# A decode block that streams its K and V cache: fourteen of the loads issued from ScalarE's queue

## The chip, the cores and the metric

The kernel runs on one core of a Trainium2 chip. A core has a matrix engine (TensorE, PE in the profile), a vector engine (VectorE, DVE), an activation engine (ScalarE, ACT), a general engine (GpSimd, POOL) and a sequencer that computes nothing (SyncE, SP). Each follows its own list of instructions in order, and they wait for each other by semaphores. Transfers between the memory of the chip (DRAM) and the core's on-chip memory are carried out by 16 DMA engines. An instruction of SP, ScalarE or GpSimd only issues a transfer; the engines do the rest. The profile tells by queue whose transfers they are: q1 holds those that SP issues, q10 those of ScalarE, q0 those of GpSimd.

The metric is the device time of one execution in microseconds, as the median of several runs.

## The reference

Two tokens (batch 2, one position each) go through an attention block that reads a cache, and then through an MLP.

```
h  = x  + attention(layernorm(x))
h2 = h  + mlp(layernorm(h))

attention: q = x @ wq                     # 512 -> 32 heads x 128
           scores = (q . k_cache) / sqrt(128)   # k_cache: 2 x 32 x 8192 x 128, fp32
           p = softmax(scores)
           o = p . v_cache                # v_cache: 2 x 32 x 8192 x 128, fp32
           o @ wo                         # 4096 -> 512
mlp:       layernorm, 512 -> 1792, gelu, 1792 -> 512, biases
```

The two caches hold 268 MB each. Everything else is small beside them: wq and wo have 8.4 MB each, the weights of the MLP 7.3 MB together.

## The kernel before

The work on the cache is cut into 32 rounds, i = 0 to 31. A round is one batch row and two heads; both heads are laid over the 128 partitions, so that a partition holds 128 keys of one head, 128 numbers each, 64 KB. One load of K, or of V, is thus 128 rows of 64 KB, 8.39 MB. There are 64 of them. They share a pool `kv` of three buffers with wq, which is loaded first; later, the weights of the MLP use the pool too. In the order of the program the buffers are taken by wq, K0, V0, K1, V1, K2 and so on, each load going into the buffer of the one three places ahead of it: V(i) takes the buffer of K(i-1), and K(i+1) takes that of V(i-1).

A round's K is worked on in four chunks. VectorE multiplies a chunk with the query in place (`multiply`, L246). GpSimd adds the two halves of each row (`halve`, L256), and VectorE sums what is left (`sums`, L266). In the last three rounds ScalarE sums some of the rows (`by_act`, L260); before those it has nothing to do there. After the fourth chunk VectorE takes the row maximum (`row_max`, L270). In the next round the maximum goes over TensorE and VectorE to all partitions (`all_max`, L273, L277, L280), ScalarE takes the exponentials (`exps`, L286 and L291), and TensorE multiplies them with V (`values`, L314, 64 matmuls). ScalarE copies the result from PSUM (`gather`, L320), TensorE sums it over partitions (`head_sum`, L335), and VectorE divides by the sum and sorts it into rows (`head_out`, L350). When the heads of a group of rows of wo are complete, they are multiplied with that group (`turned`, L367).

Two of the waits matter here. The load of V(i) is issued when the last sums over K(i-1) are done. The load of K(i+1) is issued when the matmuls over V(i-1) are done.

Within a round the program issues, in this order: the load of V(i) (L394); the exponentials, the matmuls over V of the round before; the load of K(i+1) (L409); in some rounds a group of wo (L414, `load_wo`); the four chunks, with `gather` behind the first. The list of a queue follows this order.

The groups of wo share one buffer. A group is loaded by SP (L140) or, where its rows are not evenly laid out, by GpSimd with an indirect DMA (L145), and the one behind it waits until the matmuls at L367 have used it. In the rounds that matter here SP loads one, at i = 9, and GpSimd one, at i = 13; GpSimd's group before that was loaded at i = 5.

All loads of K and V are issued by SP. ScalarE issues a single transfer, that of x at the start (L66).

Of the kernel before, what the change touches and what calls it, by code (L numbers as in the profile page):

```python
# [37 lines left out]
FAR = 4096  # L38


@with_exitstack
def tile_decode_block(ctx: ExitStack, tc: tile.TileContext, x, k, v, wq, wo, w1, b1, w2, b2, out):
    nc = tc.nc
# [23 lines left out]

    def load(src, i, parts):  # L70
        m, b = divmod(i, B)
        t = kv.tile([P, NS, DH], F32, name="kv", tag="kv")
        rows = src[b, QG * m:QG * m + QG].rearrange("h (p j) d -> (h p) j d", j=NS)
        for s0, n in parts:
            nc.sync.dma_start(t[:, s0:s0 + n], rows[:, s0:s0 + n])
        return t

    wqt = kv.tile([P, DC, H * DH], F32, name="wqs", tag="kv")
# [16 lines left out]
    for blocks in PLAN:  # L95
        shut = blocks if isinstance(blocks, tuple) else None
        r = WR if shut else blocks
        n = (P - 4 * len(shut or ())) * r
# [13 lines left out]
    for _, _, _, blocks in groups:  # L112
        if blocks and blocks not in index:
# [3 lines left out]
            for p in sorted(set(ends)):  # L117
                if ends.count(p) == 1:
                    if p in blocks:
                        edge, step, first = p, FAR, p  # L120
                    else:
                        edge, step = p, first - p - FAR
                    one = work.tile([P, 1], F32, name="ix1")
# [261 lines left out]
    next_load = 0  # L385
    free_from = 1
    kt[0] = load(k, 0, cut(1))
    for i in range(NI):
        m, b = divmod(i, B)
        done = i - 1  # L390
        late = i == NI - 1
        if not late:
            if i < NI - 2:
                vt[i] = load(v, i, cut(1))  # L394
        else:
            vt[i] = load(v, i, [(0, 64), (64, 32), (96, 24), (120, 8)])
            b1r = rows2[:, 0].rearrange("p r q -> p (r q)")[:, :FN]
            nc.vector.memset(b1r, 0.0)
            b2s = rows2[:B, 1].rearrange("b r q -> b (r q)")
            for e in range(B):  # L400
                nc.sync.dma_start(b1r[WB * e::32], b1.rearrange("(n f) -> n f", n=NG))
            nc.sync.dma_start(b2s, b2[None, :].to_broadcast([B, D]))
# [248 lines left out]
```

## Time and profile before

| what | value |
|---|---|
| median of 3 runs | 1307.52 us (1307.45 to 1307.59) |
| span of the profiled execution | 1305.9 us |
| bytes moved by DMA | 561.50 MB |
| mean rate over the span | 430 GB/s |
| VectorE busy | 932.7 us |
| GpSimd busy | 494.2 us |
| TensorE busy | 446.8 us |
| ScalarE busy | 98.6 us |

The profile is one execution. Its span goes from the first to the last instruction; the time of a run has 1.6 us more, by the median. In the lists of groups and waits a line like L246 is a line of the kernel. In the timeline a row gives the start in us, the duration in us, the engine, the line, the operation, and the tiles written and read; `x2` says that two instructions are merged, and the bracket gives the idle time before it and what ended it. `SPq` and `ACTq` are the queues' own instructions, the issuing of a transfer among them. In the DMA view a queue's row gives packets, MB and share of the 16 engines' time in the window.

### The profile page before, as it was taken

Reading aid. Unit: us, or ns where it says so; the run is one execution under the profiler, and the core shown is the slowest. Engines: PE = TensorE matmul, PEld = TensorE weight load, DVE = VectorE, ACT = ScalarE, POOL = GpSimd, SP = SyncE. Lnnn points to the kernel's source line nnn. Section 1 sums busy time; section 2 is a strip of 40 time slices with the busy share of each in tenths; the row PEclk is TensorE's granted clock in tenths of the full one; section 3 lists DMA queues with packets and bytes.
Section 4 is the critical chain, followed back from the end, with each engine's and each line's share of the span. In section 5 each row is a group of like instructions: output and inputs, shape, how many; then the busy total and the mean of one; then the engine's idle time right before and its main releaser. Section 6 shows DMA issues by size and latency. Waiting matters only on the chain.

```text
span 1305.9 us, 7466 instructions
## 1 busy us (share of the span) xinstructions
PE 446.8 (34%) x2934; PEld 130.9 (10%) x2934; DVE 932.7 (71%) x551; ACT 98.6 (8%) x431; POOL 494.2 (38%) x151
## 2 busy tenths in 40 slices
PE   3033313333332334413342232333323334123468
PEld 0001001010010101001010010101001011000113
DVE  3666688757688666787766787666787667797891
ACT  0000000000000000000000000000000000004440
POOL 0433344532344432444332454333444433453330
PEclk9566556766566666656766566666666666566689
DMA  9999999999999999999999999999999999999998
GB/s 418 426 440 428 438 422 444 424 440 426 442 426 440 428 438 428 426 444 430 436 426 438 430 434 436 424 442 424 440 426 432 438 432 436 429 428 429 428 434 351
DMA packets 12727, 561.50 MB, mean 430 GB/s; under 512 B 1568, under 2 KB 1584, under 8 KB 2484
## 3 DMA queue, kind: packets, MB, share of 16 engines
q1 hardware_dynamic: 11968, 557.08, 98.8%
q0 software_dynamic: 720, 3.93, 0.7%
q8 instruction: 23, 0.38, 0.1%
q14 instruction: 12, 0.10, 0.0%
q10 hardware_dynamic: 4, 0.00, 0.0%
HBM read 562.32 MB, written 0.00 MB: 431 GB/s over the span
## 4 chain that ended last, share of the span: by engine, by line
DMA 43%; DVE 24%; issue 14%; PE 12%; POOL 5%; ACT 1%; SPq 0%; POOLq 0%; DVEq 0%
DMA kv<-in_A_k_cache_dram 38%; DVE kv L246 14%; PE so L314 10%; DVE s L266 9%; POOL kv L256 5%; DMA kv<-in_A_v_cache_dram 3%; DMA ws<-in_B_w_dram 1%; ACT pt L291 1%; PE rowacc L367 1%; DVE orow L350 1%; PE sm L280 1%; PE sm L273 0%; DVE gm L277 0%; DVE mx L270 0%; ACT nb L286 0%
## 5 line engine op out<-in xcount | busy, mean ns | idle before, releaser
L246 DVE TENSOR_TENSOR kv<-kv,qps 128x4096 f32<-128x4096 f32 x128 | 562.4, 4415 | 313.8 <-DMA kv<-in_A_k_cache_dram 313.6
L256 POOL TENSOR_TENSOR kv<-kv 128x2048 f32<-128x2048 f32 (+3 forms) x128 | 476.8, 3734 | 754.1 <-DVE kv L246 566.3
L266 DVE TENSOR_REDUCE s<-kv 128x32 f32<-128x2048 f32 (+5 forms) x160 | 325.3, 2066 | 10.9 <-POOL kv L256 10.6
L314 PE MATMUL so<-kv,pt 128*8 128x512 f32 x2048 | 280.8, 709 | 42.7 <-ACT pt L291 37.3
L273 PE MATMUL sm<-ident,mx 128*1 128x128 f32 x32 | 10.9, 340 | 446.0 <-DVE mx L270 446.0
L314 PEld LDWEIGHTS so<-kv,pt 128*8 128x8 f32 x2048 | 56.4, 101 | 239.5 <-issue 194.3
L367 PE MATMUL rowacc<-wog,ot 128*2 128x512 f32 x70 | 50.3, 881 | 64.8 <-DVE ot L365 33.4
L286 ACT ACTIVATE nb<-sm 128x2 f32<-128x2 f32 x32 | 5.5, 172 | 851.4 <-PE sm L280 851.4
L231 PE MATMUL qps<-q,pick 2*64 2x256 f32 x64 | 13.8, 577 | 127.6 <-DVE kv L246 127.6
L273 PEld LDWEIGHTS sm<-ident,mx 128*1 128x1 f32 x32 | 2.5, 79 | 472.5 <-issue 278.0
L358 PE MATMUL sm<-ident,orow 2*128 2x2 f32 x35 | 5.2, 244 | 130.1 <-DVE orow L350 130.1
L320 ACT ACTIVATE ss<-so 128x512 f32<-128x512 f32 x31 | 18.5, 598 | 269.6 <-PE so L314 269.6
L260 ACT ACTIVATE kv<-kv 128x128 f32<-128x128 f32 x114 | 33.5, 295 | 24.2 <-DVE kv L246 21.4
L335 PE MATMUL sm<-ss,selr 128*34 128x128 f32 x240 | 28.7, 273 | 0.0
L291 ACT ACTIVATE pt<-s,nb 64x128 f32<-64x128 f32 x64 | 25.5, 399 | 1.4
L335 PEld LDWEIGHTS sm<-ss,selr 128*34 128x34 f32 x240 | 25.1, 112 | 0.0
L260 ACT ACTIVATION_READ_ACCUMULATOR kv<-kv 128x1 f32 x114 | 21.3, 186 | 0.0
L280 PE MATMUL sm<-gm,ones 1*128 1x2 f32 x64 | 16.6, 326 | 11.9 <-DVE gm L277 11.9
L277 DVE TENSOR_REDUCE gm<-sm 1x2 f32<-1x128 f32 x32 | 8.9, 279 | 16.2 <-PE sm L273 16.2
L231 PEld LDWEIGHTS qps<-q,pick 2*64 2x64 f32 x64 | 5.5, 192 | 136.9 <-DVE kv L246 133.2
L358 PEld LDWEIGHTS sm<-ident,orow 2*128 2x128 f32 x35 | 4.4, 207 | 132.6 <-DVE orow L350 79.9
L367 PEld LDWEIGHTS rowacc<-wog,ot 128*2 128x2 f32 x70 | 6.8, 107 | 97.9 <-issue 64.1
(110 smaller groups left out, 169.2 us busy)
## 6 DMA issues: line engine op xcount, KB each, us to landing
kv<-in_A_k_cache_dram SPq DMA_DIRECT2D x4, 4096.0 KB, 32.9
ws<-in_B_w_dram SPq DMA_DIRECT2D x3, 1792.0 KB, 18.5
kv<-in_A_v_cache_dram SPq DMA_DIRECT2D x1, 4096.0 KB, 33.4
wog<-in_A_wo_dram SPq DMA_DIRECT2D x3, 1024.0 KB
kv<-in_A_v_cache_dram SPq DMA_DIRECT2D x1, 2048.0 KB, 37.9
kv<-in_A_v_cache_dram SPq DMA_DIRECT2D x1, 1536.0 KB, 41.2
ws<-in_B_w_dram SPq DMA_DIRECT2D x1, 1024.0 KB, 17.0
wog<-in_A_wo_dram SPq DMA_DIRECT2D x1, 512.0 KB
```

What stands on the lines that cost most here:

```text
L231: nc.tensor.matmul(t[e * HP:(e + 1) * HP, :, b], pick[32 * n:32 * n + B, b, :], rows[:, :, e], start=True, stop=True)
L246: return nc.vector.tensor_tensor(kc, kc, qb, op=ALU.mult)
L256: nc.gpsimd.tensor_tensor(t[:, :, :DH // 2], t[:, :, :DH // 2], t[:, :, DH // 2:], op=ALU.add)
L260: nc.scalar.activation(kt[i][:, j, :], kt[i][:, j, :], AF.Copy, accum_out=ST[i][:, j:j + 1])
L266: nc.vector.tensor_reduce(ST[i][:, a:e], kt[i][:, a:e, :d], axis=AX.X, op=ALU.add)
L273: nc.tensor.transpose(MT[i], mx, ident)
L280: GI[i] = nc.tensor.matmul(GM[i], ones[:1, :], gm, start=True, stop=True)
L291: nc.scalar.activation(ptz[i % 2][ps, :, 4 * e:4 * e + 4], s[ps], AF.Exp, bias=nb[ps, e:e + 1], scale=SCALE, accum_out=LT[m][ps, 32 * e + ...
L314: m = nc.tensor.matmul(so[32 * n:32 * n + 4 * QG], ptz[i % 2][:, u, :], vt[i][:, 4 * u:4 * u + 4, :], start=(u < NG), stop=(u >= NS // 4 - ...
L320: return nc.scalar.activation(SS[i], so2[i % 2], AF.Copy)
L335: nc.tensor.matmul(OP[m], sel_row[:, j, B - 1 - c:B - 1 - c + QR], SS[i - 1 + c][:, j * DH:(j + 1) * DH], start=(c == 0 and j == 0), stop= ...
L367: nc.tensor.matmul(rowacc, t[:, r, :], wo_g[g][:, r, :], start=False, stop=(g == len(groups) - 1 and r == n - 1))
```

## The change

The function `load` counts its calls. Calls 13 to 26, counted from 0 in the order of the program, issue their transfer on ScalarE's queue; all others issue it on SP's, as before. The calls are K0, V0, K1, V1, ..., so that numbers 13 to 26 are V6, K7, V7, K8, ..., V12, K13: seven loads of V and seven of K. Each of them is one transfer of the whole 8.39 MB. Nothing else is changed: buffers, order of the program and waits are the same.

```
+BY_ACT = range(13, 27)
...
+    loads = [0]
+
     def load(src, i, parts):
         m, b = divmod(i, B)
         t = kv.tile([P, NS, DH], F32, name="kv", tag="kv")
         rows = src[b, QG * m:QG * m + QG].rearrange("h (p j) d -> (h p) j d", j=NS)
+        queue = nc.scalar if loads[0] in BY_ACT else nc.sync
+        loads[0] += 1
         for s0, n in parts:
-            nc.sync.dma_start(t[:, s0:s0 + n], rows[:, s0:s0 + n])
+            queue.dma_start(t[:, s0:s0 + n], rows[:, s0:s0 + n])
         return t
```

## The prediction

> **What bounds the kernel now.** I read the page from the top: first the busy shares, then the slices of DMA, then who waits for whom, and then single loads in the timeline.
>
> ```profile
> span 1305.9 us, 7466 instructions
> DMA  9999999999999999999999999999999999999998
> q1 hardware_dynamic: 11968, 557.08, 98.8%
> 20.00:1290.00 1270.00, 434.09 (x2736) 124.57 (x2736) 918.05 (x439) 94.28 (x425) 492.88 (x142) 0.65 1.00 432
> DVE kv L246 <- DMA kv<-in_A_k_cache_dram: 313.6, 31, 28.5
> SPq L75 <- DVE mx L270: 764.5, 28, 29.7
> ```
>
> The fourth line is a view by stage, from 20 to 1290 us: its last two columns are the DMA share and GB/s. The 16 DMA engines are busy for 1.00 of the stage and move 432 GB/s, nearly all of it on q1, the ring that SP feeds. VectorE is busy for 918 of 1270 us and waits 313.6 us for K, about 10 us in each of 31 rounds. So the bytes bound the kernel, and a change can cost time only where the engines run empty, or gain where the same bytes move faster. SP is no bound: its longest wait is for VectorE to free a buffer. (I name the row maximum that its wait is put down to; the issue comes as the last sum over K ends.)
>
> Unit prices follow from this. A load of K or V is 128 rows of 64 KB, 8.39 MB: at 432 GB/s 19.4 us, eight packets on each of 16 engines, 2.43 us each. The load that meets empty rings at the start of the run is dearer:
>
> ```profile
> 0.74 0.40 SPq L79 DMA_DIRECT2D wqs<-in_A_wq_dram  x1
> 0.74 0.54 ACTq L66 DMA_DIRECT2D x<-in_A_x_dram  x1
> wqs<-in_A_wq_dram SPq DMA_DIRECT2D x1, 22.5
> q10 hardware_dynamic: 4, 0.00, 6.2%
> ```
>
> Wq has the size of one load and takes 22.5 us from issue to landing, 3.1 us more than in a full stream. The last line is from the DMA view of 1.6 to 1.8 us: the four packets of x, ScalarE's only transfer (ring q10), start there, about 0.9 to 1.0 us after their issue at 0.74.
>
> **The change, part by part.** Counted in program order, loads 13 to 26 are V6, K7, V7 and so on to V12 and K13. Removed from SP: 14 issues of 0.33 us, 4.6 us. SP waits hundreds of us, so this gains nothing. Added to ScalarE: the same 14, at 0.33 to 0.54 us. What stands behind each on ScalarE:
>
> ```profile
> 267.46 0.33 SPq L75 DMA_DIRECT2D kv<-in_A_v_cache_dram  x1
> 269.25 0.17 ACT L286 ACTIVATE nb<-sm 128x2 f32<-128x2 f32 x1 [26.99 <-PE sm L280]
> 279.39 0.33 SPq L75 DMA_DIRECT2D kv<-in_A_k_cache_dram  x1
> 279.40 0.60 ACT L320 ACTIVATE ss<-so 128x512 f32<-128x512 f32 x1 [8.94 <-PE so L314]
> ```
>
> V6 would be issued at 267.46; the next ScalarE instruction can start only at 269.25, when the maximum has come back from TensorE, so the issue is covered by 1.8 us of idle time. K7 and the gather at L320 are released together by the same matmuls; the gather goes 0.33 to 0.54 us later, and its PSUM bank is overwritten only by the values two rounds later, a round being some 39 us. Nothing, then, in either case. The waits keep their order too: on ScalarE the buffer of a V load comes free before the exponentials of that round, and that of a K load just before the gather, so no instruction is queued behind a later event than before.
>
> What is left is that q1 and q10 both hold loads at two places: K6 (SP) with V6 (ScalarE), and K13 (ScalarE) with V13 (SP). On one ring a load waits for the one ahead of it. On two rings the trace shows what happens when GpSimd's ring q0 gets 8 KB rows of Wo while q1 is full:
>
> ```profile
> 232.77 1.16 POOL L145 DMA_INDIRECT wog<-in_A_wo_dram,ix  x1 [0.28 <-POOL wog L144]
> DMA packets 32, 1.11 MB, mean 398 GB/s; under 512 B 8, under 2 KB 8, under 8 KB 8
> q1 hardware_dynamic: 16, 1.05, 86.4%
> q0 software_dynamic: 16, 0.07, 5.7%
> ```
>
> The last three lines are the DMA view of 239.2 to 242.0 us. In 2.8 us, the time of one 64 KB and one 8 KB packet, q1 starts 16 packets and q0 starts 16: one of each on 16 engines. The rings take turns packet by packet, and q0 does not wait for q1's queued load. So with equal packets V6 takes half of the engines' time from K6.
>
> The Trainium skill (DMA: Bandwidth & Descriptors, Queues, rings and completion order) says that each DMA engine goes round robin over the queue rows, and that it drains a whole packet, roughly 9 to 17 descriptors, before it switches. The trace agrees on the turns; but here a turn is a single 64 KB row. By packets of nine descriptors an engine's eight rows of K6 would be one turn, K6 would not be delayed, and the sum would be 0.
>
> ```profile
> 280.83 8.75 DVE L246 TENSOR_TENSOR kv<-kv,qps 128x4096 f32<-128x4096 f32 x2 [12.25 <-DMA kv<-in_A_k_cache_dram]
> 310.16 0.33 SPq L75 DMA_DIRECT2D kv<-in_A_v_cache_dram  x1
> 310.16 0.29 DVE L270 TENSOR_REDUCE mx<-s 128x1 f32<-128x128 f32 x1
> 319.47 8.76 DVE L246 TENSOR_TENSOR kv<-kv,qps 128x4096 f32<-128x4096 f32 x2 [8.27 <-DMA kv<-in_A_k_cache_dram]
> ```
>
> First place. V6's first packet is due about 1.0 us after 267.46, at 268.5. K6 has landed by 280.83: 12.3 us, five packets to an engine, of which one is under way and four have not begun. Each of the four lets one packet of V6 ahead, so K6 comes 4 x 2.43 = 9.7 us late. The bytes are the same, so V6 and K7, in line on q10, still land when they did; K7 by 319.47. But VectorE works on K6 from 280.83 to 310.16, 29.3 us, and only then is the buffer for V7 free. V7's issue moves from 310.16 to 319.9, after K7 has landed: the rings are empty. It costs what Wq cost: landing at 319.9 + 22.5 = 342.4. Before, it followed K7 on a full ring: 319.47 + 19.4 = 338.9. **The loss is 3.5 us**, and in a kernel bound by bytes nothing gives it back; K8 and all behind it move by as much. What is late next is only this one round: K7 waits for VectorE instead of the reverse, and at K8 the 10 us of idle time are there again.
>
> Bounds of that term: if an engine has its next packet already committed, three turns, 7.3 us late, issue 317.5, loss 1.1 us (or none, as the engines' last packets still run then); if V6 comes in quicker, five turns, 12.1 us, loss 5.9 us. I take four turns, as 1.0 us is a measured start and anything from 0.2 less to 2 us more gives four for the slowest engine.
>
> ```profile
> 544.85 0.33 SPq L75 DMA_DIRECT2D kv<-in_A_v_cache_dram  x1
> 554.34 8.75 DVE L246 TENSOR_TENSOR kv<-kv,qps 128x4096 f32<-128x4096 f32 x2 [8.55 <-DMA kv<-in_A_k_cache_dram]
> 582.36 0.28 DVE L270 TENSOR_REDUCE mx<-s 128x1 f32<-128x128 f32 x1
> 595.13 8.75 DVE L246 TENSOR_TENSOR kv<-kv,qps 128x4096 f32<-128x4096 f32 x2 [11.66 <-DMA kv<-in_A_k_cache_dram]
> ```
>
> Second place, in the clock of before. V13's first packet at 545.9, K13 landed by 554.34: 8.4 us, one packet under way and at most three to come, 7.3 us late. V14 is then issued at 589.7 and would land at 612.2 from empty rings, but K14 is in transit to about 595 and the full stream would have landed V14 at 614.5. Covered by 2.3 us: 0. With four turns (9.7 us) it would cost 0.1 us. The margin is larger than at the first place because V13 is issued 9.5 us before K13 lands, not 13.4, and because this round carries Wo rows of GpSimd as well.
>
> The only other load that moves is a 1 MB group of Wo (L140), on SP. It now stands behind K6 and not behind K10:
>
> ```profile
> 382.14 5.87 PE L367 MATMUL rowacc<-wog,ot 128*2 128x512 f32 x8 [6.75 <-issue]
> 399.50 0.42 SPq L140 DMA_DIRECT2D wog<-in_A_wo_dram  x1
> ```
>
> Its buffer is free at 388.0, so it goes 11.5 us earlier, in turns with K9: at most five packets of 8 KB (0.30 us each) are let in, 1.5 us, against the 8 us and more for which VectorE waits for each K in the rows above. Same bytes: 0.
>
> **Sum.** 0 + 0 + 3.5 + 0 + 0 = 3.5 us on a profiled span of 1305.9 us: 1309.4. Outside the span lie 1.6 us (the median of the runs is 1307.5), so 1311.0.
>
> **Rivals.**
>
> Nothing changes (1307.5 to 1308.6). For it: only three turns, or an engine that keeps to the ring it has begun, and then VectorE's idle time covers the delay; up to 8 us of it is free. Against it: q0's packets alternate from 237 us on, 4.5 us after an issue that itself takes 1.2 us. The skill's second rule (same page, Issuing engines are not separate DMA queues) says that issuing on several engines saves only the sequencer's issue time; no wait here is for that, so by it the time would stay 1307.5.
>
> More than forecast. Five turns give 5.9 us, 1313.4. If q10 got all of the engines until V6 was through, K6 would be 19.4 us late, the loss 13.2 us, 1320.7; the even turns of q0 speak against that.
>
> Faster: two rings hide the gap between one packet and the next. For it:
>
> ```profile
> DMA packets 230, 7.23 MB, mean 441 GB/s; under 512 B 48, under 2 KB 48, under 8 KB 48
> ```
>
> That is 237.2 to 253.6 us, with q0 and q1 both at work: 441 GB/s against 432, 2%. If a second ring brought 2% for all 14 loads (14 x 19.4 = 272 us), 5.4 us would be gained, 1302.1. It decides only if it outweighs the 3.5 us and holds where q10 works alone. Against it: packets are counted whole in the window in which they start, half a packet per engine is 0.5 MB, 7% of 7.23; and for most of the 14 loads one ring alone has work.
>
> **How the numbers follow.** About 0.2% (2.6 us) is what a measurement of this kernel tells from no change. The forecast, four turns, has 0.45, and its own range is 1310.0 to 1311.6: an engine that ends K7 last idles some 2 us less than one that ends it first. Nothing changes: 0.34. More than forecast: 0.15. Faster: 0.06, of which 0.01 stays within 0.2%. Slower: 0.15 and nearly all of 0.45, with 0.01 of the forecast inside the bound: 0.59. Same: 0.34 + 0.01 + 0.01 = 0.36. Faster 0.05. The range goes from just under no change, 1307.2, to five turns, 1313.4.
>
> **What the profile will show.** Right: a second ring, q10, with some 117 MB (14 x 8.39); VectorE's first product of K6 near 290.5, not 280.83; V7 issued near 320 by ScalarE; a dip of DMA there and none elsewhere; K13 about 7 us late, without a dip; the Wo group at L140 near 390. Wrong: K6 still at 280.8 (no turns), or a dip at the second place, or a DMA share under 1.00 all the way from V6 to K13, which would make q10 itself slower.

## The result, and the profile after

The changed kernel takes 1384.4 us (median of five runs, 1381.3 to 1385.4) against 1307.5 us (1307.5 to 1307.9) for the kernel before: 1.0581 times as long, with a 95% interval of 1.0570 to 1.0593. That is 76.9 us where 3.5 us were forecast. The profiled span grew from 1305.9 to 1382.6 us.

First the page of the changed kernel: the slices of DMA, the two rings, and the costliest group of VectorE. (The change adds five lines to the file, so that L75, L246, L270 and L314 of before are L80, L251, L275 and L319 here.)

```profile
DMA  9999999997967966999799999999999999999998
GB/s 423 427 425 448 428 425 433 442 430 300 395 287 320 406 284 281 425 425 387 304 425 450 427 427 427 442 434 429 440 429 433 426 439 434 433 432 424 428 430 339
q1 hardware_dynamic: 9952, 439.64, 73.7%
q10 hardware_dynamic: 2020, 117.45, 19.9%
L251 DVE TENSOR_TENSOR kv<-kv,qps 128x4096 f32<-128x4096 f32 x128 | 562.5, 4414 | 374.7 <-DMA kv<-in_A_k_cache_dram 374.6
```

The 14 loads are on q10, 117.45 MB with the transfer of x (the prediction named some 117). But the DMA engines, full from end to end before, now run at 281 to 406 GB/s in the slices from 311 to 553 us (34.6 us each), and at 387 and 304 GB/s from 622 to 691 us. VectorE waits 374.6 us for K where it waited 313.6. Both stand idle more: neither has become the bound. The view by stage says how empty the engines run (the columns after the window's length are the busy times of PE, PEld, DVE, ACT and POOL, then the granted clock, the DMA share and GB/s), first over a long stretch, then in three holes:

```profile
360.00:600.00 240.00, 55.76 (x385) 17.06 (x374) 131.97 (x56) 7.00 (x24) 72.53 (x20) 0.61 0.81 347
340.00:348.00 8.00, 5.45 (x26) 1.50 (x30) 8.00 (x4) 0.00 (x0) 2.38 (x2) 0.50 0.01 2
384.00:398.00 14.00, 0.00 (x0) 0.00 (x0) 14.00 (x6) 0.00 (x0) 6.33 (x2) 0.50 0.26 112
440.00:450.00 10.00, 0.00 (x0) 0.00 (x0) 10.00 (x5) 0.00 (x0) 4.87 (x2) 0.50 0.02 7
```

The first of these rows in the kernel before:

```profile
360.00:600.00 240.00, 80.82 (x510) 23.77 (x506) 175.83 (x80) 11.10 (x37) 95.54 (x28) 0.66 1.00 433
```

In the first and the third hole hardly anything is moved. In the second the transfers run out: from 388 us on the share is 0.00. VectorE is busy in all three without a break. That suggests that a load is not issued because it waits for VectorE. Which one, the timelines of ScalarE's queue and of VectorE say. In ScalarE's, every row shown is the issue of a load, K8, V8, K9, V9 and K10 (`...` stands for rows left out):

```profile
348.31 0.34 ACTq L80 DMA_DIRECT2D kv<-in_A_k_cache_dram  x1
...
354.13 0.34 ACTq L80 DMA_DIRECT2D kv<-in_A_v_cache_dram  x1
...
398.20 0.33 ACTq L80 DMA_DIRECT2D kv<-in_A_k_cache_dram  x1
...
398.60 0.41 ACTq L80 DMA_DIRECT2D kv<-in_A_v_cache_dram  x1
...
450.79 0.33 ACTq L80 DMA_DIRECT2D kv<-in_A_k_cache_dram  x1
```

```profile
290.48 8.75 DVE L251 TENSOR_TENSOR kv<-kv,qps 128x4096 f32<-128x4096 f32 x2 [21.88 <-DMA kv<-in_A_k_cache_dram]
...
348.31 0.29 DVE L275 TENSOR_REDUCE mx<-s 128x1 f32<-128x128 f32 x1
...
370.13 8.75 DVE L251 TENSOR_TENSOR kv<-kv,qps 128x4096 f32<-128x4096 f32 x2 [15.57 <-DMA kv<-in_A_k_cache_dram]
...
398.20 0.29 DVE L275 TENSOR_REDUCE mx<-s 128x1 f32<-128x128 f32 x1
...
450.80 0.29 DVE L275 TENSOR_REDUCE mx<-s 128x1 f32<-128x128 f32 x1
...
638.36 8.75 DVE L251 TENSOR_TENSOR kv<-kv,qps 128x4096 f32<-128x4096 f32 x2 [23.10 <-DMA kv<-in_A_k_cache_dram]
...
708.84 8.75 DVE L251 TENSOR_TENSOR kv<-kv,qps 128x4096 f32<-128x4096 f32 x2 [8.85 <-DMA kv<-in_A_k_cache_dram]
```

K8 is issued at 348.31, and at 348.31 VectorE takes the row maximum of K7: its last sums over K7 have just ended. K9 goes at 398.20, with the maximum of K8 at 398.20; K10 at 450.79, with that of K9 at 450.80. K11, K12 and K13 do the same at 501.97, 552.30 and 610.59. In the kernel before, K8 was issued when the matmuls over V6 were done. SP's queue and TensorE there:

```profile
322.88 0.33 SPq L75 DMA_DIRECT2D kv<-in_A_k_cache_dram  x1
```

```profile
313.12 9.69 PE L314 MATMUL so<-kv,pt 128*8 128x512 f32 x64 [1.29 <-ACT pt L291]
```

313.12 + 9.69 = 322.81, and the issue follows at 322.88. The profile prints no buffer numbers, but these times say that the load of K(i+1) now goes into the buffer of K(i), which VectorE still works on, and not into that of V(i-1). Transfer and use of K no longer overlap.

The next load of V is held back too. V9 is issued at 398.60, right behind K9. Its buffer can only be that of V7, since the matmuls over V8 begin at 410.27, and the matmuls over V7 had ended at 365.17:

```profile
356.42 8.75 PE L319 MATMUL so<-kv,pt 128*8 128x512 f32 x64 [1.29 <-ACT pt L296]
```

So V9 could have filled the engines, but it stands behind the waiting K9 in ScalarE's list.

One round is then K8's way from empty engines, 348.31 to 370.13, 21.8 us, and VectorE's work on it, 370.13 to 398.20, 28.1 us: 49.9 us in place of 38.7 us. The rows of the kernel before, for K9 and K15 (K8 was first used at 358.24):

```profile
396.94 8.75 DVE L246 TENSOR_TENSOR kv<-kv,qps 128x4096 f32<-128x4096 f32 x2 [8.16 <-DMA kv<-in_A_k_cache_dram]
...
633.84 8.75 DVE L246 TENSOR_TENSOR kv<-kv,qps 128x4096 f32<-128x4096 f32 x2 [8.59 <-DMA kv<-in_A_k_cache_dram]
```

There are six such rounds, of 50 to 59 us: from the first use of K7 (319.55 us, before 319.47) to that of K13 (638.36, before 554.34), 84.0 us more in all. In the two longest, SP issues a load beside the one that is waited for: V13 at 566.10 beside K12, K14 at 629.37 beside K13. About 9 us come back behind K13: K15 is first used at 708.84 us here and at 633.84 us before, 75.0 us late. What is left of the 76.9 us comes behind it.

TensorE's list has changed too. The rows of the changed kernel in which the matmuls over V6 come:

```profile
342.55 1.96 PE L236 MATMUL qps<-q,pick 2*64 2x256 f32 x6 [20.44 <-DVE kv L251]
344.44 9.61 PE L319 MATMUL so<-kv,pt 128*8 128x512 f32 x64
```

They stand behind the spreading of the next query (L236), whose tile VectorE frees with its last product over K7. So V6's buffer comes free near 354, not at 322.8, and V8 is issued at 354.13. The program's order is not the order of the lists, then. Neither the buffers nor these orders are written in the kernel. The framework that builds it orders each engine's list and hands out the pool's buffers itself, and here it did both otherwise than before. This document calls the two together the plan.

### The profile page after: what moved, and what is told of

It is laid out like the page before. It is cut to its first block, busy times and chain, and to the rows that moved or that the text cites. A ratio compares the mean times of both kernels' runs of the same rounds, so it can differ in the third digit from the quotient of the medians.

```text
span 1382.6 us, 7451 instructions
## 1 busy us (share of the span) xinstructions
PE 449.1 (32%) x2934; PEld 133.0 (10%) x2934; DVE 932.2 (67%) x551; ACT 98.6 (7%) x431; POOL 494.4 (36%) x151
## 3 DMA queue, kind: packets, MB, share of 16 engines
q10 hardware_dynamic: 2020, 117.45, 19.9%
## 4 chain that ended last, share of the span: by engine, by line
DMA 44%; DVE 31%; PE 9%; issue 9%; POOL 5%; ACT 1%; SPq 0%; POOLq 0%; DVEq 0%
DMA kv<-in_A_k_cache_dram 40%; DVE kv L251 18%; DVE s L271 12%; PE so L319 8%; POOL kv L261 5%; DMA kv<-in_A_v_cache_dram 3%; DMA ws<-in_B_w_dram 1%; PE rowacc L372 1%; ACT pt L296 1%; DVE orow L355 1%; PE sm L285 0%; PE sm L278 0%; DVE gm L282 0%; DVE mx L275 0%; ACT nb L291 0%
## 5 line engine op out<-in xcount | busy, mean ns | idle before, releaser
L251 DVE TENSOR_TENSOR kv<-kv,qps 128x4096 f32<-128x4096 f32 x128 | 562.5, 4414 | 374.7 <-DMA kv<-in_A_k_cache_dram 374.6
L319 PE MATMUL so<-kv,pt 128*8 128x512 f32 x2048 | 275.7, 698 | 38.3 <-ACT pt L296 34.7
L319 PEld LDWEIGHTS so<-kv,pt 128*8 128x8 f32 x2048 | 56.5, 100 | 231.3 <-issue 190.6
L236 PE MATMUL qps<-q,pick 2*64 2x256 f32 x64 | 14.4, 570 | 150.2 <-DVE kv L251 150.2
L340 PE MATMUL sm<-ss,selr 128*34 128x128 f32 x240 | 32.9, 292 | 77.5 <-ACT ss L325 77.5
L325 ACT ACTIVATE ss<-so 128x512 f32<-128x512 f32 x31 | 18.5, 597 | 482.1 <-PE so L319 288.8
L236 PEld LDWEIGHTS qps<-q,pick 2*64 2x64 f32 x64 | 5.7, 189 | 158.6 <-DVE kv L251 154.8
L149 POOL MEMSET wog<- 128x2048 f32 x5 | 9.0, 1804 | 24.5 <-PE rowacc L372 24.5
L355 DVE TENSOR_SCALAR orow<-sm,rlr 2x128 f32<-2x128 f32 (+7 forms) x45 | 14.0, 346 | 5.6 <-PE sm L340 5.3
```

The source lines that it names most:

```text
L236: nc.tensor.matmul(t[e * HP:(e + 1) * HP, :, b], pick[32 * n:32 * n + B, b, :], rows[:, :, e], start=True, stop=True)
L251: return nc.vector.tensor_tensor(kc, kc, qb, op=ALU.mult)
L319: m = nc.tensor.matmul(so[32 * n:32 * n + 4 * QG], ptz[i % 2][:, u, :], vt[i][:, 4 * u:4 * u + 4, :], start=(u < NG), stop=(u >= NS // 4 - ...
L325: return nc.scalar.activation(SS[i], so2[i % 2], AF.Copy)
L340: nc.tensor.matmul(OP[m], sel_row[:, j, B - 1 - c:B - 1 - c + QR], SS[i - 1 + c][:, j * DH:(j + 1) * DH], start=(c == 0 and j == 0), stop= ...
L355: nc.vector.tensor_scalar(orow[g % 2][:B, :r, p0:p0 + run].rearrange("b r p -> b p r"), OP[h // QG][r0e:r0e + B, c0:c0 + run * r].rearrang ...
```

## The experiments

The theory (A in the expectations) is that the plan costs the time, its buffers and its order, and that the transfers on two rings cost only a few microseconds, as predicted. Against it stands (B) that the loads cost the time themselves, on ScalarE or on its ring q10. The experiments write the plan of before into the kernel, as a whole or in parts, or move fewer loads. All of them compute the whole reference.

Two edits are used throughout. **Buffers held**: each load names its buffer, in the rotation of before, and so do wq and the weights of the MLP.

```
-    kv = ctx.enter_context(tc.tile_pool(name="kv", bufs=BUFS))
+    kv = ctx.enter_context(tc.tile_pool(name="kv", bufs=1))
...
-        t = kv.tile([P, NS, DH], F32, name="kv", tag="kv")
+        t = kv.tile([P, NS, DH], F32, name="kv", tag=f"kv{(loads[0] + 1) % 3}")
```

**Order held**: from round 5 to round 16 each engine's instructions are chained in the order of the program. The chain is meant to add no wait between engines; both_sp shows what it costs.

```
+        if i == 4:
+            mark = len(nc.cur_bb.bb.instructions)
+        if i == 16:
+            before = {}
+            for ins in nc.cur_bb.bb.instructions[mark:]:
+                if ins.engine in before:
+                    tc.add_manual_dep(ins, before[ins.engine].name, mybir.DependencyInfo(
+                        mybir.DependencyClass.NoSync, mybir.DependencyReason.DATA), reason="order")
+                before[ins.engine] = ins
```

| kernel | loads on ScalarE | held | median, us | over before, us | ratio and 95% interval |
|---|---|---|---|---|---|
| changed kernel | V6 to K13 | nothing | 1384.4 | +76.9 | 1.0581 (1.0570 to 1.0593) |
| both_sp | none | buffers, order | 1307.7 | 0.0 | 1.0000 (0.9991 to 1.0009) |
| both_act | V6 to K13 | buffers, order | 1313.2 | +5.5 | 1.0045 (1.0031 to 1.0059) |
| both_k7 | K7 to K13 | buffers, order | 1308.4 | +0.8 | 1.0006 (0.9997 to 1.0015) |
| both_alt | V6, V7, ... V12 | buffers, order | 1320.2 | +12.5 | 1.0102 (1.0087 to 1.0117) |
| chain_act | V6 to K13 | order | 1346.5 | +38.7 | 1.0296 (1.0279 to 1.0314) |
| pe_act | V6 to K13 | TensorE's order | 1383.1 | +75.3 | 1.0576 (1.0558 to 1.0593) |
| fix_act | V6 to K13 | buffers | 1377.3 | +69.5 | 1.0537 (1.0520 to 1.0555) |
| v6only | V6 | nothing | 1313.4 | +5.6 | 1.0043 (1.0026 to 1.0060) |
| n4 | V6, K7, V7, K8 | nothing | 1328.4 | +20.6 | 1.0161 (1.0144 to 1.0178) |
| k7free | K7 to K13 | nothing | 1381.2 | +73.5 | 1.0569 (1.0551 to 1.0587) |

Each is compared with runs of the kernel before on the same chip, whose medians were 1307.5 us for the changed kernel and 1307.7 to 1307.8 us for the others.

### both_sp: the plan held, nothing moved

```
-BY_ACT = range(13, 27)
+BY_ACT = range(0, 0)
```
and both edits above.

> Control: all loads on SP as before, but every load has its buffer fixed by its number (three tags of one buffer each) and the instructions of rounds 5 to 16 are chained in the order of the program on each engine. If fixing costs nothing by itself, 1307.5 us within 0.1%. If it costs something, the other runs with the same fixing are to be read against this one.

1307.7 us, as the kernel before. Holding the plan costs nothing by itself, so the next kernels show the move alone.

### both_act: the plan held, all fourteen moved

Both edits above, and nothing else beside the change.

> The change with buffers and order fixed as in the control. Theory A (the 77 us come from other buffers and another order that the framework chose once the loads stood on ScalarE, not from the ring): only the turns of K6 with V6 are left, K6 is used near 290.5, V7 is issued near 320, one dip of the DMA, 1310 to 1312 us. Theory B (a load issued by ScalarE, or two rings in use, is slow by itself): the rounds from 8 to 13 still last 50 us, near 1384 us.

1313.2 us: 5.5 of the 76.9 us remain, about 1 us above the upper end that theory A gave. The same fourteen loads are on the same ring, so ScalarE and q10 are not the cause of the other 71 us. The slices of its page, and the long stretch by stage:

```profile
GB/s 416 434 428 442 422 444 422 438 426 376 440 423 444 420 444 424 438 432 428 436 432 430 434 434 428 440 428 434 438 424 432 436 430 437 425 439 424 430 427 347
```

```profile
360.00:600.00 240.00, 68.37 (x444) 19.96 (x440) 173.37 (x79) 10.50 (x36) 95.26 (x27) 0.65 1.01 434
```

One dip is left, 376 GB/s in the tenth slice, 295 to 328 us: 32.8 us x (432 - 376) / 432 = 4.3 us of transfer missing, a rough figure, as neighbouring slices differ by some 20 GB/s. From 360 to 600 us the share is 1.01 where the changed kernel had 0.81.

### both_k7: the plan held, without V6

```
-BY_ACT = range(13, 27)
+BY_ACT = range(14, 27)
```
and both edits.

> As the run before, but the range begins one load later, at K7 (13 loads, K7 to K13). Then V6 shares with K7 and it is V that comes late, which nothing waits for until 310. Theory A: no K load is late at the first place, K6 used near 280.8, no dip, 1307.5 to 1308.2 us. Theory B: near 1370 us, as 13 of 14 loads are still ScalarE's. A third reading, that any change of ring costs some us, expects the same 1310 to 1312 us as the run before.

1308.4 us, 0.8 more than before, with an interval that takes in no change. K6 has no second ring beside it, and VectorE starts on it at 281.64 (280.83 before):

```profile
281.64 4.42 DVE L251 TENSOR_TENSOR kv<-kv,qps 128x4096 f32<-128x4096 f32 x1 [12.61 <-DMA kv<-in_A_k_cache_dram]
```

So what both_act loses goes with V6 beside K6. The other thirteen loads on ScalarE cost nothing that can be measured.

### both_alt: the plan held, the loads of V alone on ScalarE

```
-BY_ACT = range(13, 27)
+BY_ACT = range(13, 26, 2)
```
and both edits. V6, V7 and so on to V12 go by q10, the loads of K by q1.

> Buffers and order fixed, V6 to V12 on ScalarE and K7 to K13 on SP, so that two rings hold loads in every one of seven rounds. If the rings share the same bytes per second without loss, only the first round pays: 1310 to 1313 us. If two rings move bytes faster by the 2% that I named as a rival, seven rounds of 38.7 us gain 5.4 us: near 1305 us. If sharing costs throughput, clearly over 1315 us.

1320.2 us: a miss. I had taken the sharing of two rings to cost once, at the first load. VectorE's first products of K10 to K13 show that it comes back:

```profile
454.14 8.75 DVE L251 TENSOR_TENSOR kv<-kv,qps 128x4096 f32<-128x4096 f32 x2 [21.79 <-DMA kv<-in_A_k_cache_dram]
...
485.58 8.75 DVE L251 TENSOR_TENSOR kv<-kv,qps 128x4096 f32<-128x4096 f32 x2 [1.26 <-DMA kv<-in_A_k_cache_dram]
...
533.08 8.75 DVE L251 TENSOR_TENSOR kv<-kv,qps 128x4096 f32<-128x4096 f32 x2 [18.17 <-DMA kv<-in_A_k_cache_dram]
...
564.52 8.75 DVE L251 TENSOR_TENSOR kv<-kv,qps 128x4096 f32<-128x4096 f32 x2 [0.86 <-DMA kv<-in_A_k_cache_dram]
```

VectorE waits about 20 us for one K and about 1 us for the next. Against the rows of before, K10 is used 18.5 us later (454.14 against 435.66), K11 8.8 us (485.58 against 476.76), K12 17.6 us and K13 10.2 us. K10, issued at 413.73, shares the engines with V9 and V10 and is late. VectorE then frees K10's buffer late, and V11 goes only at 483.29; until then K11 has the engines to itself once V10 is through, and catches up. K12 shares again. The stretches of the view by stage:

```profile
360.00:600.00 240.00, 77.91 (x468) 21.95 (x464) 172.64 (x78) 10.50 (x36) 95.44 (x27) 0.62 0.98 421
483.00:514.00 31.00, 11.27 (x75) 2.85 (x75) 28.71 (x13) 1.75 (x6) 15.39 (x4) 0.61 0.96 408
514.00:533.00 19.00, 12.27 (x85) 4.12 (x85) 0.35 (x2) 1.75 (x6) 0.00 (x0) 0.77 1.02 439
```

A time over 1315 us was to mean that sharing costs throughput. The rows speak against that: from 514 to 533 us, with K12 and V12 both in transit, the engines are full and move 439 GB/s. The loss lies where they are not full, as around the late issue of V11 (share 0.96). At 1320.2 us two rings are no gain either: the rival "faster" finds no support here.

### chain_act: the order held, the buffers free

Only the second edit.

> The change with the order fixed (rounds 5 to 16, as in the control) and the buffers left to the framework. It now gives K8, K10 and K12 the buffer that VectorE must still finish (the K before), and K9, K11 and K13 the one of V. Theory A, with the cost in the buffers: three slow rounds and not six, each some 11 to 12 us over 38.7, on top of the 5.5 us of the fixed run: 1345 to 1352 us. If the cost lies in the order, near 1313 us.

1346.5 us, as theory A had it. ScalarE's queue issues the loads in their written order, but the framework still hands out the buffers. ScalarE's queue with the issues of K8, K9 and K10, and VectorE's row maxima of K7 and K9:

```profile
349.12 0.34 ACTq L80 DMA_DIRECT2D kv<-in_A_k_cache_dram  x1
...
360.75 0.34 ACTq L80 DMA_DIRECT2D kv<-in_A_k_cache_dram  x1
...
439.48 0.33 ACTq L80 DMA_DIRECT2D kv<-in_A_k_cache_dram  x1
```

```profile
349.12 0.29 DVE L275 TENSOR_REDUCE mx<-s 128x1 f32<-128x128 f32 x1
...
439.48 0.29 DVE L275 TENSOR_REDUCE mx<-s 128x1 f32<-128x128 f32 x1
```

K8 (349.12) and K10 (439.48) wait for the row maximum of the K before; K9 (360.75) does not. K12 does again, at 529.14. With three such loads in place of six, half of the loss is gone.

### pe_act: TensorE's order held alone

In the chain, `if ins.engine != mybir.EngineType.PE: continue` stands ahead of the test, so that TensorE's list alone is chained.

> The change with the order fixed on TensorE alone, buffers left to the framework. All six loads K8 to K13 still get the buffer of the K before. If the cost lies in the buffers, six slow rounds: 1378 to 1388 us, as the change. If it lies in TensorE's order (the values of round 6 stand behind the new query), near 1313 us.

1383.1 us, no better than the changed kernel. Yet TensorE's list is mended:

```profile
322.53 8.97 PE L319 MATMUL so<-kv,pt 128*8 128x512 f32 x64 [1.29 <-ACT pt L296]
331.44 1.08 PE L236 MATMUL qps<-q,pick 2*64 2x256 f32 x8
```

The matmuls over V6 come ahead of the query again, 22 us sooner than in the changed kernel, and nothing is gained: K does not wait for them any more. K8 is issued at 348.75 with VectorE's maximum of K7, as in the changed kernel, and K9 to K13 wait in the same way.

### fix_act: the buffers held, the order free

Only the first edit.

> The change with the buffers fixed and the order left to the framework. Its list for ScalarE has V8 ahead of K8, V10 ahead of K10 and V12 ahead of K12, and V waits for the last sums over the K before. If a load held back until these sums costs the same whether by its buffer or by its place in the queue, three slow rounds: 1343 to 1352 us. If only the buffers count, near 1313 us.

1377.3 us, a miss: the right buffers alone give back 7 us, not half. ScalarE's queue shows why:

```profile
348.38 0.33 ACTq L80 DMA_DIRECT2D kv<-in_A_v_cache_dram  x1
353.81 0.33 ACTq L80 DMA_DIRECT2D kv<-in_A_k_cache_dram  x1
```

```profile
389.69 8.75 DVE L251 TENSOR_TENSOR kv<-kv,qps 128x4096 f32<-128x4096 f32 x2 [35.44 <-DMA kv<-in_A_k_cache_dram]
...
490.56 8.75 DVE L251 TENSOR_TENSOR kv<-kv,qps 128x4096 f32<-128x4096 f32 x2 [41.20 <-DMA kv<-in_A_k_cache_dram]
```

The framework has put V8 (348.38) ahead of K8 (353.81). Both are in one queue and on one ring, so K8 comes behind 8.39 MB that nobody needs yet, and is used at 389.69, 35.9 us after its issue. (K8's own issue waits for the matmuls over V6, which end at 353.74, because TensorE's list is the changed one here too; V8 has the ring until 370.2 in any case.) Two rounds, K8 to K10, take 490.56 - 389.69 = 100.9 us where they took 77.4 (358.24 to 435.66). K8 is used 31.5 us later than before, K10 54.9, K12 75.0; behind K12 some of it comes back, and 69.5 us remain. I had expected three slow rounds of some 12 us each; a pair of rounds with V ahead of K loses 20 us and more.

### v6only: one load moved, nothing held

```
-BY_ACT = range(13, 27)
+BY_ACT = range(13, 14)
```

> Nothing fixed, only load 13 (V6) on ScalarE. Buffers of the loads are as before, and the lists of the engines differ in a reciprocal and some row copies of VectorE. By the turns alone K6 is 9.7 us late and the loss is that of the fixed run, 1310 to 1313.5 us; if ScalarE's issue itself brings the framework to plan badly, several times that.

1313.4 us, the loss of both_act, without any help to the plan. A single load moved leaves the buffers of the loads and their waits as they were, and one pair of rings that share, V6 with K6, costs the same 5.6 us.

### n4: four loads moved, nothing held

```
-BY_ACT = range(13, 27)
+BY_ACT = range(13, 17)
```

> Nothing fixed, only loads 13 to 16 (V6, K7, V7, K8) on ScalarE. In the framework's list one load of K, K8, waits for VectorE's last sums over the K before; all others wait for TensorE as before. Theory A: the turns (5.5 us) and one slow round of 11 to 12 us: 1322 to 1327 us. If slow rounds come from ScalarE's loads as such, two rounds have them: over 1330 us.

1328.4 us, 1.4 us above the upper end expected. One K load, K8, waits for VectorE. It goes out on ScalarE's ring at 348.28, with the row maximum of K7 at 348.28; V8 follows on SP's ring at 354.43:

```profile
348.28 0.33 ACTq L80 DMA_DIRECT2D kv<-in_A_k_cache_dram  x1
```

```profile
354.43 0.33 SPq L80 DMA_DIRECT2D kv<-in_A_v_cache_dram  x1
```

```profile
382.12 8.75 DVE L251 TENSOR_TENSOR kv<-kv,qps 128x4096 f32<-128x4096 f32 x2 [27.25 <-DMA kv<-in_A_k_cache_dram]
```

K8 takes until 382.12, 33.8 us, where it took 21.8 us with V8 behind it on its own ring. The two rings share here as well. Counting this kernel with those above, the loss goes with the number of K loads that wait for VectorE: none, 5.5 us (both_act); one, 20.6; three, 38.7 (chain_act); six, 75.3 and 76.9 (pe_act and the changed kernel). Over the 5.5 us that is 15.1 us for the one that shares its transfer, 11.1 us each for three, and 11.6 to 11.9 us each for six.

### k7free: K6 not disturbed, nothing held

```
-BY_ACT = range(13, 27)
+BY_ACT = range(14, 27)
```

> Nothing fixed, the range begins one load later, at K7 (13 loads). With buffers and order fixed this cost 0.8 us. The framework's list again has K8 to K13 waiting for the sums over the K before. Theory A: six slow rounds without the turns at the first place: 1370 to 1382 us. If the bad plan costs only where K6 is late on the chip, near 1308 us.

1381.2 us. V6 is back on SP, and the loss is nearly whole. So the late K6 does not set the slow rounds off; the plan has them without it.

## Why the prediction was wrong, point by point

**The bound.** Right: the bytes bound the kernel before, and time is lost only where the DMA engines run empty. The dips and holes above are read in that way.

**The step that failed** is in the costing of the move to ScalarE: "The waits keep their order too: on ScalarE the buffer of a V load comes free before the exponentials of that round, and that of a K load just before the gather, so no instruction is queued behind a later event than before." It took the buffers and the order of every engine from the trace of before. In the changed kernel the buffer of K8 comes free at 348.31, with the end of VectorE's work on K7, and V9 is queued behind the later event that K9 waits for. The section on the change said the same as the prediction, "buffers, order of the program and waits are the same". That holds for the text of the program, not for what is built from it. Six loads of K were given the buffer of the K before them, and each then waits for VectorE: 71.4 of the 76.9 us, by both_act against the changed kernel. No rival named this, and the range, up to 1313.4, left it out. Of the two parts, holding the order alone gives back 38.2 us and the buffers alone 7.4 us, both together 71.4: they are not a sum, since either of them left free puts some loads of K behind something late.

**Fourteen issues at nothing.** Right for the issue itself: in both_k7 thirteen of them come to 0.8 us, which can't be told from none.

**Turns packet by packet, K6 late by 9.7 us.** Right in size. VectorE's first product of K6 was forecast near 290.5 and comes at 290.48 in the changed kernel, at 290.44 in both_act. The turns are a little less even than forecast: from 268 to 285 us of the changed kernel q1 starts 60 rows of 64 KB and q10 52. The reading of the trace of before was too simple in one point: of the 16 packets of q0 between 239.2 and 242.0 us eight are under 512 B, so that window shows eight rows of 8 KB, not 16. Between 244.4 and 249.2 us, though, q0 starts 31 packets, at most four of them that small, beside 30 of q1. The prediction set against this the rule of the Trainium skill (DMA: Bandwidth & Descriptors, Queues, rings and completion order) that an engine drains a whole packet, roughly 9 to 17 descriptors, before it switches. By that rule K6 would still have come at 280.8; these runs do not bear it out for rows of 64 KB.

**The first place, 3.5 us.** The mechanism is right, the size too small. In both_act V7 is issued at 319.77 (forecast 319.9). VectorE's rows for K8 in both_act, then in the kernel before:

```profile
362.68 8.75 DVE L251 TENSOR_TENSOR kv<-kv,qps 128x4096 f32<-128x4096 f32 x2 [12.75 <-DMA kv<-in_A_k_cache_dram]
...
566.56 8.75 DVE L251 TENSOR_TENSOR kv<-kv,qps 128x4096 f32<-128x4096 f32 x2 [16.32 <-DMA kv<-in_A_k_cache_dram]
599.35 8.75 DVE L251 TENSOR_TENSOR kv<-kv,qps 128x4096 f32<-128x4096 f32 x2 [3.65 <-DMA kv<-in_A_k_cache_dram]
```

```profile
358.24 8.75 DVE L246 TENSOR_TENSOR kv<-kv,qps 128x4096 f32<-128x4096 f32 x2 [9.58 <-DMA kv<-in_A_k_cache_dram]
```

K8 is 4.4 us late: the term was 3.5. The price of a load that meets empty rings was taken from wq, 22.5 us. The DMA views give what V7 took from issue to landing, in both_act (319 to 322 us) and in the kernel before (309 to 311 us):

```profile
kv<-in_A_v_cache_dram ACTq DMA_DIRECT2D x1, 23.5
```

```profile
kv<-in_A_v_cache_dram SPq DMA_DIRECT2D x1, 28.6
```

It lands at 319.77 + 23.5 = 343.3, against 310.16 + 28.6 = 338.8 before (forecast 342.4 against 338.9). So the term was too small by that one price. It is no fixed one: V7 took 22.2 us in the changed kernel, and K8 21.8. The whole kernel loses 5.5 us. The last 1 us comes later in the run (K19 is still 4.2 us late, K26 5.7), and no run here settles from what.

**The second place, nothing.** Right, in both_act. K13 is used at 566.56 there, 12.2 us after the 554.34 of before; less the 4.4 us by which all is late (K14, at 599.35, is 4.2 us late), 7.8 us. The forecast was 7.3. K14 is back in line, and the slices show no dip there.

**The group of Wo, nothing.** Issued at 391.84 in both_act, forecast near 390, and no trace of a cost. In the changed kernel, where all is late, it goes at 408.75.

**The rivals.** "Nothing changes" needed three turns or none; K6 at 290.5 excludes it. "Faster" needed 2% from a second ring; both_alt, where two rings hold loads in seven rounds, is not faster, nor is both_k7. "More than forecast" named five turns (1313.4) and a q10 that comes first (1320.7); what came is above both by far, and by another mechanism.

What the profile would show was told before: a dip there "and none elsewhere", and, as a sign of a failure, a share under 1.00 all the way to K13. From 360 to 600 us the share is 0.81, as the sign said; the reading that went with it, that q10 itself is slower, does not hold, since both_act moves 434 GB/s with the same loads on q10.

**What stays open.** Why the framework hands out other buffers when it finds more than one load on ScalarE wasn't settled: the traces show the lists and the buffers that came out, not the estimates behind them. One moved load does not do it (v6only), four do (n4), and K6's delay is not the reason (k7free).

## What to carry to other kernels

Where a framework orders the lists and hands out buffers, moving an instruction to another queue is a new plan and not a move: before anything is costed, compare each engine's list and what each load waits for, and write the plan down in the kernel if the move is to be tried alone. A load that takes the buffer of the operand just in use turns overlap into a sum, here 50 us and more a round for 38.7, and it holds back the loads behind it in its queue; in the profile it shows as an issue at the very time of the last instruction over that operand, with the DMA engines empty before it. And a load on a second ring takes turns with the load that somebody waits for: change rings where nobody waits, as with K7 in both_k7.

## What the runs showed of the hardware

Two full rings share nearly evenly by rows of 64 KB: from 268 to 285 us of the changed kernel q1 starts 60 of them and q10 52, and K6 came 9.7 us late, four packets of 2.43 us. The Trainium skill (DMA: Bandwidth & Descriptors, Issuing engines are not separate DMA queues) says that issuing on several engines saves only the sequencer's issue time. The runs agree that it brings no speed: both_act moves 434 GB/s from 360 to 600 us, the kernel before 433. But it was not free: 5.6 us for one load (v6only), 12.5 us with the loads of V and K on different rings (both_alt). What I had not expected is that last number: the delay does not die out after one round but comes again in every second one: K10 is 18.5 us late, K11 8.8, K12 17.6, K13 10.2.
